# Lightning attention, then a highway layer, on one core: q, k and v loaded in DMAs of 256 KB instead of 128 KB, and five more idle matrix products near the start

## The chip, the cores and the metric

The kernel runs on one NeuronCore of a Trainium2 chip. The metric is the device time of one execution, in microseconds; the kernel before was run three times. A profile of one execution goes with it. Its times are counted from the first instruction, and it names the engines PE (TensorE, matrix products), PEld (TensorE's weight loads), DVE (VectorE), ACT (ScalarE), POOL (GpSimd) and SP (SyncE, which here only issues DMAs). "SPq" and the like mean an engine's sequencer.

## The reference

Four batches, eight heads, 768 positions, 64 features a head. Attention with decay runs over blocks of 64 positions, with a state per batch and head; its output goes through a highway layer of width 512.

```python
for b in range(nb):                      # blocks of 64 positions
    intra = (qb @ kb.T * Dmask) @ vb     # Dmask[i, j] = lam ** (i - j) for i >= j, else 0
    inter = (qb * lam ** (pos + 1)) @ kv_state
    out[block] = intra + inter
    kv_state = lam ** 64 * kv_state + (kb * lam ** (63 - pos)).T @ vb
H = relu(x @ w_h)                        # x: out as [3072, 512]
T = sigmoid(x @ w_t + b_t)
result = T * H + (1 - T) * x
```

## The kernel before

The work is cut into 12 steps: four batches of three steps, each of 256 positions and all eight heads (N = 12, NST = 3). A step is loaded as three float32 tensors q, k and v of 512 KB each (`load`, L205 to L209). Steps 0 and 1 are handled in two parts of four heads, p0 and p1 (`PARTS`, L41); the later ones whole. A partition holds two neighbouring positions, so that one run of a load is 512 bytes of HBM; 128 KB are two heads, 128 partitions each, 256 runs.

The chain of a step is this. Casts to bfloat16 make kb from k (`cast_k`, L212), and qb and vs from q and v with powers of lam multiplied in (`scale`, L215). PE turns kb and qb (`trans`, L220), ACT or DVE copies the turned tiles out of PSUM to kT and qT (`evac_h`, L225). PE makes the scores (`scores`, L233), DVE masks them to m (`mask`, L242). PE multiplies m with vs (`intra`, L257, tile o), adds the share of the state (`inter`, L247, called i0 below for a batch's first step), and advances the state in tile kv (`state`, L268), which ACT or DVE copies to ss (`evac_s`). Tile o is copied to xT (`evac_x`). The highway layer takes xT: eight products with a half of w_h or w_t make one group (`block`, L290, four groups a step), DVE makes hmx (`hmx`, L296), ACT the sigmoid, DVE and POOL the product th (`thmx`, L308). PE turns xT + th back (`turn`, L311), a copy brings it to o_sb, and SP stores it (`store`, L322; 25 stores).

The weights come in eight DMAs of 256 KB (`load_w`, L168) that SP issues after the loads of step 2, and they are cast in pieces of 128 x 512.

`fill` (L196) is an idle product: two matmuls of the identity with 512 columns each into a PSUM tile that no one reads. The kernel issues twelve at the start (`NF`, L40), ahead of the first turn.

What runs where is fixed. Every piece of work is a task with an engine (`FIXED` and `EN`), and `ORDER` lists the tasks; each engine, SP's queue among them, gets its own in that order, one after the other. In SP's queue all loads stand ahead of all stores. Each tensor has a small ring of buffers: five for a step's q, k and v in float32 (`LA`), four for parts, twelve for o_sb (`OB`), three for kb and vs, two for qb.

Of the kernel before, what the change touches and what calls it, by code (L numbers as in the profile page):

```python
# [20 lines left out]
class Task:  # L21
# [15 lines left out]
XB = 3  # L37
OB = 12
WB = 5
NF = 12  # L40
PARTS = 2  # L41
TH = ["DVE", "POOL"]
GROUPS = [[0], [1], [2], [3], [4], [5], [6], [7], [8], [9], [10]]
# [1 line left out]
    cw="GVGGGAAA", ck2="VVGA", cq2="VVGG", cv2="VGVV", et2="VAAVAVAV", ss="AAVAAAAVAVAAAAVVAVAV", xT="VAVAAAAAAAAAAAAAAAAAAAAA",  # L45
    eo="AVVAAAVAAVAVAVAAAAVAVA", ck="VAAGGAGVGG", cq="GVGGGGGGGG", cv="GGGGGGGGGG", et="AVAVAVVAVAAAAAAAAAAA", eo1="A", eo3="AA")
ORDER = [
    34, 32, 20, 33, 21, 43, 22, 42, 23, 16, 44, 24, 25, 26, 83, 27, 35, 17, 28, 82, 37, 29, 30, 36, 92, 31, 46, 38, 40, 93, 39,
    41, 84, 45, 50, 48, 51, 47, 52, 94, 49, 53, 86, 55, 133, 54, 56, 85, 132, 57, 88, 95, 134, 90, 18, 89, 58, 91, 96, 12, 59, 19,
    64, 60, 63, 87, 61, 107, 65, 100, 97, 14, 62, 108, 102, 98, 109, 99, 136, 103, 0, 101, 104, 105, 106, 110, 135, 2, 111, 138,  # L50
    8, 140, 112, 139, 10, 137, 141, 113, 6, 13, 4, 114, 15, 145, 142, 171, 146, 115, 1, 73, 147, 143, 170, 123, 3, 74, 172, 9,
    144, 211, 124, 148, 66, 149, 7, 11, 150, 71, 5, 210, 67, 68, 72, 116, 174, 69, 212, 151, 121, 70, 152, 117, 75, 251, 173, 178,
    122, 118, 153, 179, 176, 175, 119, 250, 154, 177, 120, 79, 76, 155, 214, 252, 185, 77, 80, 180, 161, 181, 186, 184, 213, 187,
    125, 289, 188, 182, 218, 189, 162, 156, 190, 183, 215, 219, 288, 216, 157, 159, 217, 158, 191, 254, 290, 160, 220, 192, 225,
    126, 221, 193, 226, 129, 253, 201, 227, 328, 127, 130, 258, 163, 256, 202, 194, 329, 257, 255, 259, 224, 195, 228, 263, 222,
    330, 229, 196, 292, 223, 230, 260, 264, 197, 231, 370, 164, 261, 291, 232, 265, 167, 233, 199, 198, 165, 293, 369, 262, 168,
    200, 266, 294, 267, 296, 331, 203, 295, 234, 407, 297, 236, 268, 332, 235, 298, 368, 237, 269, 303, 334, 299, 238, 270, 241,
    333, 304, 406, 271, 239, 305, 335, 336, 240, 242, 373, 204, 408, 300, 205, 337, 302, 306, 272, 307, 301, 243, 448, 308, 207,
    338, 273, 372, 208, 343, 309, 344, 339, 447, 277, 310, 345, 311, 274, 410, 278, 446, 279, 275, 244, 371, 280, 276, 319, 487,
    245, 409, 342, 320, 346, 281, 340, 374, 347, 341, 488, 376, 348, 411, 375, 317, 377, 312, 486, 412, 313, 247, 413, 349, 318,  # L60
    450, 81, 378, 248, 381, 350, 314, 379, 351, 382, 414, 449, 315, 206, 383, 352, 415, 451, 316, 282, 380, 353, 283, 249, 384,
    452, 385, 321, 454, 453, 386, 285, 416, 284, 490, 286, 387, 455, 169, 421, 417, 354, 422, 388, 287, 389, 423, 357, 489, 246,
    355, 128, 359, 491, 358, 209, 390, 356, 360, 78, 494, 391, 166, 361, 420, 495, 424, 131, 418, 322, 425, 419, 397, 426, 325,
    323, 492, 398, 326, 324, 362, 427, 327, 493, 456, 461, 395, 457, 428, 462, 429, 365, 463, 363, 460, 396, 366, 364, 464, 458,
    465, 499, 367, 392, 459, 466, 435, 500, 393, 501, 430, 394, 496, 431, 399, 467, 432, 436, 468, 497, 469, 437, 433, 498, 438,
    434, 502, 400, 503, 439, 472, 401, 504, 470, 402, 473, 403, 471, 505, 404, 474, 440, 506, 405, 477, 441, 520, 475, 442, 478,
    507, 476, 443, 509, 508, 479, 444, 512, 510, 521, 445, 513, 514, 511, 523, 522, 515, 480, 483, 524, 516, 481, 528, 484, 526,
    525, 482, 529, 531, 485, 527, 517, 532, 530, 518, 533, 534, 519, 535, 536]


@with_exitstack
def kernel(
# [11 lines left out]
    nc = tc.nc  # L84
    B, H, S, D = q.shape
    C = 128
# [4 lines left out]
    J = 2  # L91
# [48 lines left out]
    def buf(name, tag, shape, dtype=BF16, bufs=1, pool=None):  # L140
        made[name] = Tile(tag, bufs)
        made[name].make = lambda: (pool or sb).tile(shape, dtype, tag=tag, name=tag, bufs=bufs)
        return made[name]

    def get(*key):
        x = made[key]
        if x.obj is None:
            x.obj = x.make()
        return x.obj

    def task(kind, emit, reads=(), writes=(), after=(), only=()):
        eng = FIXED.get(kind)
        if eng is None:
            i = count.get(kind, 0)
            count[kind] = i + 1
            eng = LETTER[EN[kind][i]]
        t = Task(kind, eng, emit, [made[x] for x in reads], [made[x] for x in writes], after, only)
        tasks.append(t)
        return t
# [40 lines left out]
    buf(("fill",), "o", [128, 2, NP, C], F32, pool=ps)  # L200
    for i in range(NF):
        task("fill", fill, writes=[("fill",)])


    def load(x, src, n, p, hs):  # L205
        b, c = divmod(n, NST)
        for h in range(hs.start, hs.stop, 2):
            nc.sync.dma_start(out=get(x, n, p)[:, h - hs.start:h - hs.start + 2, :],  # L208
                              in_=src[b, h:h + 2, c * 2 * C:(c + 1) * 2 * C, :].rearrange("h (p j) d -> p h (j d)", j=J))  # L209


    def cast_k(n, p, hs, eng):  # L212
# [115 lines left out]
    for n in range(N):  # L328
        bt, c = divmod(n, NST)
# [18 lines left out]
        for p, hs in enumerate(parts):  # L348
            z = hs.stop - hs.start
            for x, src in (("k", k), ("q", q), ("v", v)):  # L350
                buf((x + "f", n, p), x + "f" + y, [128, z, J * D], F32, 4 if P2 else LA)
                task("l" + y, lambda eng, x=x, src=src, n=n, p=p, hs=hs: load(x + "f", src, n, p, hs), writes=[(x + "f", n, p)])
            for x in "kq":
                buf((x + "tr", n, p), "w", [128, z // 2, J, C], bufs=WB, pool=ps)
            cast = {}
            cast["k"] = task("ck" + y, lambda eng, n=n, p=p, hs=hs: cast_k(n, p, hs, eng), reads=[("kf", n, p)], writes=[("kb", n)])
            cast["q"] = task("cq" + y, lambda eng, n=n, p=p, hs=hs: scale("qf", get("qb", n).rearrange("p j h d -> p h j d"), pow_q, n, p, hs, eng),
                             reads=[("qf", n, p)], writes=[("qb", n)], after=[pows])
            task("cv" + y, lambda eng, n=n, p=p, hs=hs: scale("vf", get("vs", n), pow_k, n, p, hs, eng), reads=[("vf", n, p)], writes=[("vs", n)], after=[pows])
            for x, xT in (("k", kT), ("q", qT)):  # L360
                task("tr" + y, lambda eng, x=x, n=n, p=p, hs=hs: trans(x, n, p, hs), reads=[(x + "b", n)], writes=[(x + "tr", n, p), xT], only=[cast[x]])
                ev[x, p] = task("et" + y, lambda eng, x=x, n=n, p=p, hs=hs: evac_h(x, n, p, hs, eng), reads=[(x + "tr", n, p)], writes=[xT])
# [111 lines left out]
```

## Time and profile before

| | us |
|---|---|
| runs of the kernel | 127.79, 126.82, 128.57; median 127.79 |
| the profiled execution, its span | 127.79, 126.0 |
| PE busy (share of the span) | 105.4 (84%) |
| DVE, ACT, POOL busy | 78.8, 73.0, 63.6 |
| first load issued, last load issued, first store issued | 0.80, 90.50, 91.06 |
| last store issued | 122.77 |
| DMA | 27.58 MB, mean 219 GB/s |

A busy time counts the engine's own instructions; waiting and issuing are not in it. The end of a matmul is modelled, so a busy PE need not be at its peak. The clock column is the share of full speed that TensorE was granted. A wait is named by what ended it: an engine with its tile and line, or a DMA by its destination and source.

### The profile page before, as it was taken

To read this page: it belongs to the slowest core of one execution; us is meant where nothing else is said; L and a number is where in the kernel's file an instruction comes from. 1 tells how busy PE (TensorE), PEld (TensorE's weight loads), DVE (VectorE), ACT (ScalarE), POOL (GpSimd) and SP (SyncE) were. 2 spreads that over 40 slices of the span, in tenths; PEclk is the share of its full clock that TensorE was granted. 3 is DMA by queue.
4 is the path that set the end of the run, shared out by engine and by line. 5 is a ranking of instruction groups with operands and counts; after the bars stand their busy time and mean duration, and the time that the engine had idled before them with its cause. 6 is when DMAs were issued, how large, how long until landed. Compare 5 with 4: busy or idle time off the path is not lost.

```text
span 126.0 us, 4886 instructions
## 1 busy us (share of the span) xinstructions
PE 105.4 (84%) x2073; PEld 88.3 (70%) x2073; DVE 78.8 (63%) x128; ACT 73.0 (58%) x137; POOL 63.6 (50%) x55
## 2 busy tenths in 40 slices
PE   5983778839999997998499986990999999999960
PEld 1442657726889886887388875890979988889950
DVE  0389648750898995988269624884347498666530
ACT  4831423364278887180596695580666872866770
POOL 6007406075099196953877995419979021030520
PEclk9999755595999999999999999999779999999996
DMA  2989968899888687857887788786899972024253
GB/s 50 259 237 261 265 187 240 230 350 314 237 252 223 193 224 206 240 160 207 243 233 219 224 213 252 219 245 199 241 337 365 380 280 92 0 88 166 88 213 123
DMA packets 45117, 27.58 MB, mean 219 GB/s; under 512 B 2980, under 2 KB 42152, under 8 KB 45096
## 3 DMA queue, kind: packets, MB, share of 16 engines
q1 hardware_dynamic: 44944, 27.27, 72.1%
q8 instruction: 16, 0.26, 0.9%
q14 instruction: 5, 0.04, 0.1%
q10 hardware_dynamic: 152, 0.01, 0.1%
HBM read 20.98 MB, written 6.29 MB: 216 GB/s over the span
## 4 chain that ended last, share of the span: by engine, by line
SPq 35%; PE 29%; DMA 19%; issue 4%; POOL 4%; DVE 4%; ACT 1%; POOLq 1%; DVEq 0%
SPq L208 35%; PE w L293 16%; DMA vf<-in_v_dram 7%; DMA kf<-in_k_dram 5%; DMA w_f<-in_moe_w_t_dram 5%; PE w L315 4%; DMA qf<-in_q_dram 2%; PE w L223 2%; PE o L264 2%; PE w L239 2%; DVE hmx L297 2%; PE kv L272 2%; POOL qb L217 2%; POOL vs L217 1%; PE o L252 1%
## 5 line engine op out<-in xcount | busy, mean ns | idle before, releaser
L293 PE MATMUL w<-xT,w_b 128*128 128x256 bf16 (+1 forms) x416 | 48.9, 271 | 0.4 <-DVE m L243 0.4
L293 PEld LDWEIGHTS <-w_b 128*128 128x128 bf16 x416 | 37.5, 100 | 5.8 <-issue 0.8
L243 DVE TENSOR_TENSOR m<-w,tri 128x512 bf16<-128x512 f32 x48 | 30.7, 685 | 6.0 <-PE w L239 5.8
L217 POOL TENSOR_TENSOR vs<-vf,pow_k 128x1024 bf16<-128x1024 f32 (+1 forms) x11 | 20.1, 1824 | 20.4 <-DMA vf<-in_v_dram 14.3
L309 POOL TENSOR_TENSOR th<-t_sb,hmx 128x512 bf16<-128x512 bf16 (+1 forms) x13 | 14.9, 1144 | 22.1 <-DVE hmx L297 14.8
L217 POOL TENSOR_TENSOR qb<-qf,pow_q 128x1024 bf16<-128x1024 f32 (+1 forms) x11 | 19.2, 1745 | 9.1 <-DMA qf<-in_q_dram 9.1
L297 DVE SCALAR_TENSOR_TENSOR hmx<-w,xT 128x512 bf16<-128x512 f32 (+1 forms) x26 | 16.5, 646 | 6.5 <-PE w L293 6.2
L173 ACT ACTIVATE kT<-w 128x1024 bf16<-128x1024 bf16 (+1 forms) x11 | 10.0, 907 | 11.8 <-PE w L223 11.8
L306 ACT ACTIVATE w<-w,bt_col 128x256 f32<-128x256 f32 (+1 forms) x26 | 11.3, 434 | 8.4 <-PE w L293 6.6
L223 PE MATMUL w<-id,kb 128*128 128x128 bf16 x96 | 8.4, 231 | 8.1 <-POOL kb L175 7.4
L272 PE MATMUL kv<-vs,kb 64*64 64x64 bf16 x320 | 10.6, 203 | 4.4 <-POOL vs L217 3.1
L239 PE MATMUL w<-qT,kT 64*64 64x128 bf16 x384 | 13.1, 232 | 1.4 <-ACT qT L173 0.7
L173 ACT ACTIVATE xT<-o 128x512 bf16<-128x512 f32 x22 | 12.1, 595 | 3.5 <-PE o L264 2.7
L315 PE MATMUL w<-id,th 128*128 128x128 bf16 x96 | 12.9, 220 | 0.6 <-POOL th L309 0.6
L272 PEld LDWEIGHTS <-kb 64*64 64x64 bf16 x320 | 9.0, 116 | 6.0 <-issue 5.8
L306 ACT ACTIVATE t_sb<-w,bt_col 128x256 bf16<-128x256 f32 (+1 forms) x26 | 10.5, 459 | 4.3 <-PE w L293 4.3
L223 PEld LDWEIGHTS <-kb 128*128 128x128 bf16 x96 | 6.2, 103 | 9.7 <-POOL kb L175 8.2
L315 PE MATMUL w<-id,xT 128*128 128x128 bf16 x96 | 12.9, 220 | 0.0
L309 DVE TENSOR_TENSOR th<-w,hmx 128x512 bf16<-128x512 f32 (+1 forms) x13 | 8.4, 649 | 7.0 <-ACT w L306 6.8
L173 ACT ACTIVATE o_sb<-w 128x512 f32<-128x512 f32 (+1 forms) x17 | 9.7, 576 | 4.4 <-PE w L315 4.2
L239 PEld LDWEIGHTS <-kT 64*64 64x64 bf16 x384 | 9.4, 113 | 2.2 <-issue 1.5
L315 PEld LDWEIGHTS <-th 128*128 128x128 bf16 x96 | 9.4, 98 | 0.9 <-POOL th L309 0.8
(46 smaller groups left out, 124.0 us busy)
## 6 DMA issues: line engine op xcount, KB each, us to landing
vf<-in_v_dram SPq DMA_DIRECT2D x48, 128.0 KB, 3.3
kf<-in_k_dram SPq DMA_DIRECT2D x48, 128.0 KB, 3.3
qf<-in_q_dram SPq DMA_DIRECT2D x48, 128.0 KB, 3.0
out_dram<-o_sb SPq DMA_DIRECT2D x23, 256.0 KB, 4.0
w_f<-in_moe_w_t_dram SPq DMA_DIRECT2D x4, 256.0 KB, 5.5
w_f<-in_moe_w_h_dram SPq DMA_DIRECT2D x4, 256.0 KB, 5.7
out_dram<-o_sb SPq DMA_DIRECT2D x2, 128.0 KB, 1.8
lam_bc<-in_lam_dram ACTq DMA_DIRECT2D x1, 4.0 KB, 2.7
```

What stands on the lines that cost most here:

```text
L173: A.activation(dst, src, AF.Copy)
L208: nc.sync.dma_start(out=get(x, n, p)[:, h - hs.start:h - hs.start + 2, :], in_=src[b, h:h + 2, c * 2 * C:(c + 1) * 2 * C, :].rearrange("h ...
L217: ENG[eng].tensor_tensor(dst[:, hs], in0=get(x, n, p).rearrange("p h (j d) -> p h j d", j=J), in1=pw[:, :, :, None].to_broadcast([128, hs. ...
L223: T.transpose(get(x + "tr", n, p)[:, i, j, :], get(x + "b", n)[:, j, h:h + 2, :], id128)
L239: T.matmul(get("s", n, u, e)[half(b), i, j, :], lhsT=turned("k", n)[half(e), hp, b * C + j:(b + 1) * C:J], rhs=turned("q", n)[half(e), hp, ...
L243: V.tensor_tensor(get("m", n, u)[:, e], in0=get("s", n, u, e), in1=tri[:, None].to_broadcast([128, 2, J, C]), op=ALU.mult)
L272: T.matmul(get("kv", n // NST)[half(e), hp, :], lhsT=get("kb", n)[half(b), j, 2 * hp + e, :], rhs=get("vs", n)[half(b), 2 * hp + e, j, :], ...
L293: T.matmul(get(x, g, js[0])[:, i, :], lhsT=w[:, kc, j * 128:(j + 1) * 128], rhs=get("xT", g)[:, kc, :], start=(kc == 0), stop=(kc == KC - 1))
L297: V.scalar_tensor_tensor(get("hmx", g, js[0]), in0=get("h", g, js[0]), scalar=0.0, in1=get("xT", g)[:, js[0]:js[-1] + 1, :], op0=ALU.max, ...
L306: A.activation(get(*gate(g, js))[:, i, :], get("t", g, js[0])[:, i, :], AF.Sigmoid, bias=bt_col[:, j:j + 1])
L309: ENG[TH[js[0] // len(js) % 2]].tensor_tensor(get("th", g)[:, js[0]:js[-1] + 1, :], in0=get(*gate(g, js)), in1=get("hmx", g, js[0]), op=AL ...
L315: T.matmul(get("x", n, b, p)[:, (j - js[0]) * 128:(j - js[0] + 1) * 128], lhsT=get(x, g)[:, j, r * C:(r + 1) * C], rhs=id128, start=(j == ...
```

## The change

Three things differ.

`load` issues one DMA for four heads (256 KB, 512 runs) instead of one for two: 72 loads instead of 144. A part of step 0 or 1 is one DMA, a whole tensor of a later step two.

`NF` is 17 instead of 12. The first twelve fills stand where they did. The five others stand on PE's queue one each after the turns of k part 0, q part 0, q part 1 and k part 1 of step 0, and after the first scores of step 0.

`ORDER` is written anew. The tasks after the fills have numbers that are five higher. Engine by engine, apart from the fills, PE's order is the same. On SP the store of step 2, half 0, goes from the tenth to the fourth place of the stores and that of step 4, half 0, from the seventh to the tenth. On DVE, xT of step 0, half 0, and the copy of the bias go behind the two casts of vs of step 1, one mask of step 1 goes behind the copy of ss and of qT, and four other tasks pass a neighbour. On ACT two tasks and on POOL one task pass a neighbour.

```diff
-NF = 12
+NF = 17
...
 ORDER = [
-    34, 32, 20, 33, 21, 43, 22, 42, 23, 16, 44, 24, 25, 26, 83, 27, 35, 17, 28, 82, 37, 29, 30, 36, 92, 31, 46, 38, 40, 93, 39,
+    39, 37, 20, 38, 21, 48, 22, 47, 23, 16, 49, 24, 25, 26, 88, 27, 40, 17, 28, 87, 42, 29, 30, 41, 97, 31, 51, 43, 32, 98, 44,
+    45, 33, 46, 89, 50, 55, 52, 34, 99, 56, 53, 35, 91, 54, 138, 57, 36, 58, 90, 137, 60, 59, 93, 100, 139, 95, 61, 18, 94, 101,
...
     def load(x, src, n, p, hs):
         b, c = divmod(n, NST)
-        for h in range(hs.start, hs.stop, 2):
-            nc.sync.dma_start(out=get(x, n, p)[:, h - hs.start:h - hs.start + 2, :],
-                              in_=src[b, h:h + 2, c * 2 * C:(c + 1) * 2 * C, :].rearrange("h (p j) d -> p h (j d)", j=J))
+        for h in range(hs.start, hs.stop, 4):
+            nc.sync.dma_start(out=get(x, n, p)[:, h - hs.start:h - hs.start + 4, :],
+                              in_=src[b, h:h + 4, c * 2 * C:(c + 1) * 2 * C, :].rearrange("h (p j) d -> p h (j d)", j=J))
```

## The prediction, written before the result was known

> **What bounds the kernel now.** I read the chain of work that ended last first, then the DMA issues, the DMA queues, and tables by stage.
>
> ```profile
> SPq 35%; PE 29%; DMA 19%; issue 4%; POOL 4%; DVE 4%; ACT 1%; POOLq 1%; DVEq 0%
> ...
> q8 instruction: 16, 0.26, 0.9%
> ...
> vf<-in_v_dram SPq DMA_DIRECT2D x48, 128.0 KB, 3.3
> kf<-in_k_dram SPq DMA_DIRECT2D x48, 128.0 KB, 3.3
> qf<-in_q_dram SPq DMA_DIRECT2D x48, 128.0 KB, 3.0
> ```
>
> The largest share of the chain is SP's sequencer, which only issues. Its timeline says why (columns: start, duration, instruction, count):
>
> ```profile
> 8.99 0.98 SPq L208 DMA_DIRECT2D kf<-in_k_dram  x2
> 10.02 0.98 SPq L208 DMA_DIRECT2D qf<-in_q_dram  x2
> 11.04 2.01 SPq L208 DMA_DIRECT2D vf<-in_v_dram  x4
> 13.09 3.37 SPq L208 DMA_DIRECT2D qf<-in_q_dram  x4
> ```
>
> From 8.99 to 13.09 are eight issues: 0.51 us each, back to back, so 128 KB per 0.51 us, 256 GB/s whatever the DMA engines could do. 144 loads and 8 weight loads make 152 x 0.51 = 78 of the 90 us before the first store (91.06). The other 12 us are long issues as in the last row (3.37 instead of 2.0). Each meets a packet of queue q8, 16 KB of instructions; 0.9% of 16 engines over 126 us is 18.1 us, 1.13 us each. It holds up one DMA engine: in the semaphore times one load lands at 14.90, the next at 17.19, and then the engine that was late catches up, nine landings to 20.61, 0.38 us each. After the weights there are eleven at 0.41 us (31.53 to 36.03). So 128 KB can pass in about 0.40 us.
>
> Next, what TensorE loses. Tables by stage (PE, PEld, DVE, ACT, POOL busy, then clock, DMA share, GB/s), then PE's waits from 27 us on:
>
> ```profile
> 11.07:14.48 3.41, 1.49 (x57) 1.36 (x57) 2.52 (x6) 1.12 (x2) 2.46 (x4) 1.00 0.92 264
> 14.48:24.72 10.24, 8.22 (x168) 6.99 (x161) 7.37 (x11) 3.27 (x6) 2.32 (x2) 0.50 0.80 221
> 31.55:89.58 58.03, 50.35 (x1086) 44.15 (x1080) 40.39 (x61) 36.26 (x66) 39.69 (x26) 1.00 0.79 222
> 89.58:92.99 3.41, 3.41 (x75) 2.71 (x73) 2.29 (x4) 2.37 (x4) 3.41 (x3) 0.50 0.86 258
> 93.00:120.00 27.00, 26.94 (x547) 24.21 (x546) 17.81 (x32) 18.25 (x39) 8.19 (x8) 1.00 0.52 192
> ```
>
> ```profile
> PE w L223 <- POOL kb L175: 5.4, 4, 3.0
> PE kv L272 <- POOL vs L217: 3.1, 2, 2.0
> PE w L239 <- ACT qT L173: 0.7, 1, 0.7
> PE w L293 <- DVE m L243: 0.4, 1, 0.4
> ```
>
> Once the loads are in (93 us), PE is full to 120: PE sets the end. Before that it waits for casts that themselves waited for loads: POOL began kb at 48.94, 56.59 and 87.17 right after k landed, vs at 25.35 and 59.66 right after v. Steps are loaded every 7.3 us (first q issue of step 3 at 25.92, of step 11 at 84.08). PE needs 6.8: turns of k for step 3 at 38.30, for step 8 at 76.42, less 4.3 us of waits between them, over 5. The loads are the slower by 0.5 us a step.
>
> **What the Trainium skill says.** "DMA: Bandwidth & Descriptors", section "Issuing engines are not separate DMA queues": the sequencer's time to start a DMA is usually small beside the DMA. Here it is not: 0.51 against 0.40 us. The same page, "Queues, rings and completion order": an engine takes queue rows in turn, a packet at a time; the q8 packets agree, as each delays a landing. "TensorE: Matmul & The Clock Gate", Part 1: after an idle window of about 3.4 us the array runs at half clock until a busy one. The rows above agree: 1.49 of 3.41 us busy, then 10.24 us at 0.50; and 3.0 us idle at 85 to 88, then 3.41 us at 0.50.
>
> **The change, part by part.**
>
> *Loads.* 72 issues fewer take 72 x 0.51 = 37 us from SP. Bytes, 512-byte runs and run count stay. What an issue with 512 runs costs, the trace doesn't show. Upper bound: in proportion to runs, 1.03 us, and nothing is won. Lower bound: as now, 0.51. For the slope: stores (128 runs) that follow a semaphore wait take 0.33 us at least, loads (256 runs) 0.37, so 0.04 per 128 runs and about 0.6 us for 512. I take 0.6: below the 2 x 0.40 = 0.80 us that the transfer lasts, so the DMA engines become the limit and SP then stalls at no cost. For the transfer I keep 0.38 below and 0.43 above (16 packets of an engine at the median record of 27 ns). A 256 KB load lands as its second half did; steps 2 to 11 wait for all of a tensor anyway, and for steps 0 and 1 a part is now one DMA. No earlier use is lost.
>
> *Landings early on.* First load: 3.93 + 0.40 = 4.33 (its pair: 4.40 now), then 0.80 each. Part k1/p0 (eighth) 9.9 against 12.21; v1/p1 (twelfth) 13.1 against 17.44; with one instruction packet, k2 17.5 against 20.61 and v2 19.1 against 25.19; the weights at 0.72 a piece (as now) and another packet, 25.9 against 31.11.
>
> *Five fills.* Each two products of 512 columns, 0.43 us from start to start at full clock: 2.15 us on PE, between 8.2 and 11.3. The twelve fills already hold PE until 7.99, though kb was ready at 5.87, so these add directly: second scores of step 0 at 11.3 instead of 10.58, DVE's four masks end about 13.5 instead of 12.76. The products of m and vs start at 13.6 instead of 13.70: they now wait for masks where the turns of k of step 1 (12.99, cast waited for its load) used to come. DVE's order also puts two casts of vs (0.69 each) ahead of xT of step 0, so xT ends at 16.1 instead of 15.08 and PE's i0 comes at 16.1 instead of 15.13. Up to here, 1.0 us lost.
>
> *Steps 1 and 2.* Three load waits go: kv of step 1 for vs (DVE idle 1.84, landing 17.44), kb of step 2 (20.61), vs of step 2 (25.19). PE is idle in 12.0 to 16.1 save 1.0 us, so I expect half clock again. On DVE's queue: masks, ss, qT and kb of step 2 end near 20.7 (now 21.64); qT of step 2 near 23.7 (24.85); scores of step 2 23.8 (24.90). POOL ends vs of step 2 at 21.0 (27.25), so kv follows at 24.2 (27.30) and the highway products at 24.7 (27.68). In the kernel before these ran at half clock from 28.14; with the gap gone they run full, and the third product group, at 31.93 now, starts at about 26.9: **5.0 us gained**. At full clock throughout, 25.8 (6.1); if DVE's queue slips, 28.5 (3.4).
>
> *Steps 3 to 11.* A step is supplied every 12 x 0.40 + 1.13 = 5.9 us, below PE's 6.8 and even at 0.43 (6.3): from step 3 the loads run ahead, with 5 buffers each. PE's waits of the list, 9.6 less 2.0 for kv of step 2 already counted: **7.6 us**. The half clock at 89.58 to 92.99, half of 3.41: **1.7 us**. New waits: POOL becomes dense, two casts of 1.90, kb 1.04 and th 1.15 = 6.0 of 6.8 us; followed through its queue from th of step 0, kb of step 8 ends near 65 and PE wants it at 67.6, so nothing stops, but the slack is thin. I add 1.0 us. Loads end near 74; the stores follow, twelve o_sb buffers against a 13th write near 83. The tail, 121.3 to 126.0, stays.
>
> *Other moves.* On SP the store of step 2, half 0, stands fourth instead of tenth, that of step 4, half 0, tenth instead of seventh; all stores stay behind all loads, and step 2's was turned at 54.5: nothing. On DVE, ACT and POOL ten instructions pass a neighbour or two (mask of step 1 behind ss, which I used above; q of step 11 ahead of a th): I count nothing, since PE's lead over them hides it; where a neighbour is late one instruction's time is lost, 0.4 to 1.9 us, which is within the 1.0 us and the first rival.
>
> Sum on the profiled span: 126.0 - 5.0 - 7.6 - 1.7 + 1.0 = 112.7. The profiled execution took 127.79, 1.8 us more than its span, and 127.79 is also the median of the three runs: 112.7 + 1.8 = **114.5 us**.
>
> **Rivals.** The forecast above has 0.51. *The early queues give less* (chance 0.2): fills and the moved xT hold DVE, the shift is 2 to 3 us and POOL's queue adds 1 more: 117.5 to 119. For it: DVE busy 7.37 of 10.24 us in that stage. *DMA limits more* (0.15): instruction packets cost the queue 2 us each, as the 14.90 to 17.19 gap did, giving 4.8 + 2.3 = 7.1 a step, above 6.8; the 7.6 us are then won by half: 118. Against it: catching up. *All early work at full clock, no new waits* (0.1): 126.0 - 6.1 - 7.6 - 1.7 + 1.8 = 112.4. *Issue in proportion to runs* (0.04; not faster): at L208 an issue of 1.03 us keeps 256 GB/s, and the fills' 1.0 us stands: 128 to 129. It decides from 0.95 us per issue (12 x 0.475 + 1.13 = 6.8). Against it: the 0.33 and 0.37.
>
> **How the numbers follow.** A measurement here tells about 2%. Faster by more: all cases but the last, 0.95; within 2%: 0.03; slower 0.02 (fills without any gain). The likeliest case alone spans 113 to 116.5 (shift 6.1 to 3.4 us, new waits 0.5 to 1.5). The range runs from 111, the full-clock case with landings at 0.38 (36 x 0.02 = 0.7 less up to v2) and the spread of the runs shown (126.82 to 128.57), to 119, which holds both middle rivals.
>
> **What would show it.** Right: 72 loads at 0.8 us from issue to issue, above 300 GB/s until about 30 us; last load landed near 74; no PE wait on kb or vs after 30 us; no half clock near 90. Wrong: issues of 1.0 us with DMA share as now; PE waiting on POOL though loads have landed; i0 far behind 16 us.

## The result and the profile after

The kernel after took 111.84 us (median of four runs, 111.70 to 112.25), beside 127.31 us for the kernel before in turn with it on the same chip: ratio 0.882, with a 95% interval of 0.874 to 0.890. Its profiled execution took 111.97 us, with a span of 110.2. Here and below a time is the median of all runs of a kernel, while a ratio with its interval rests on the runs within 1.5% of a kernel's fastest.

On the page of the kernel after, these rows answer to the chain by engine and to the DMA issues (their count, size, median us from issue to landing):

```profile
PE 71%; SPq 12%; DMA 6%; POOL 5%; issue 1%; DVE 1%; POOLq 1%; ACT 0%
...
vf<-in_v_dram SPq DMA_DIRECT2D x24, 256.0 KB, 6.0
kf<-in_k_dram SPq DMA_DIRECT2D x24, 256.0 KB, 5.5
qf<-in_q_dram SPq DMA_DIRECT2D x24, 256.0 KB, 5.4
```

SP's sequencer has gone from 35% of the chain to 12%, and PE from 29% to 71%. A load takes longer from issue to landing (5.4 to 6.0 us instead of 3.0 to 3.3): it carries twice the bytes and, with the DMA engines kept busy, stands in their queue. SP's timeline of the kernel after shows the two kinds of issue:

```profile
1.30 0.51 SPq L208 DMA_DIRECT2D kf<-in_k_dram  x1
1.86 1.05 SPq L208 DMA_DIRECT2D qf<-in_q_dram  x2
2.95 1.43 SPq L208 DMA_DIRECT2D kf<-in_k_dram  x1
...
10.58 1.71 SPq L208 DMA_DIRECT2D qf<-in_q_dram  x2
12.33 1.71 SPq L208 DMA_DIRECT2D kf<-in_k_dram  x2
```

The second to fourth, with little in the queue yet, take 0.51 us each (0.55 from start to start), although each carries 512 runs. Later it is 0.88 us from one to the next (10.58 to 12.33 for two), at a DMA share above 1.1: SP is held up by the transfer. The stages of the kernel after, with columns as before (PE, PEld, DVE, ACT, POOL busy, clock, DMA share, GB/s), and its PE waits from 24 us on:

```profile
11.07:14.48 3.41, 2.71 (x80) 1.83 (x81) 3.02 (x6) 1.33 (x3) 2.40 (x3) 1.00 1.22 290
14.48:24.00 9.52, 6.29 (x220) 5.11 (x209) 8.31 (x15) 4.93 (x9) 4.15 (x3) 1.00 1.11 299
31.00:90.00 59.00, 58.76 (x1341) 52.48 (x1339) 46.60 (x73) 45.41 (x81) 46.80 (x31) 1.00 0.99 288
```

```profile
PE w L315 <- POOL th L309: 0.6, 1, 0.6
PE w L223 <- POOL kb L175: 0.2, 1, 0.2
```

From 31 to 90 us PE is busy in 58.76 of 59.00; in the kernel before it was 50.35 of 58.03 over about the same stretch. The waits for kb, vs and qT are gone but for 0.2 us. What the DMA engines moved rose from 222 to 288 GB/s (284 from 31 to 72 us, while only loads were issued).

### The profile page after: what moved, and what is told of

Its sections match the earlier page's. It is cut to its first block, busy times and chain, and to the rows that moved or that the text cites. A ratio compares the mean times of both kernels' runs of the same rounds, so it can differ in the third digit from the quotient of the medians.

```text
span 110.2 us, 4797 instructions
## 1 busy us (share of the span) xinstructions
PE 100.9 (91%) x2083; PEld 84.4 (77%) x2083; DVE 78.5 (71%) x128; ACT 73.2 (66%) x137; POOL 63.9 (58%) x55
## 4 chain that ended last, share of the span: by engine, by line
PE 71%; SPq 12%; DMA 6%; POOL 5%; issue 1%; DVE 1%; POOLq 1%; ACT 0%
PE w L293 37%; SPq L208 12%; PE w L315 9%; PE w L223 8%; DMA vf<-in_v_dram 6%; PE o L264 5%; PE w L239 4%; PE kv L272 4%; PE o L252 3%; POOL vs L217 2%; POOL qb L217 2%; POOL kb L175 1%; DVE hmx L297 1%; POOLq L469 1%; ACT o_sb L173 0%
## 5 line engine op out<-in xcount | busy, mean ns | idle before, releaser
L293 PE MATMUL w<-xT,w_b 128*128 128x256 bf16 (+1 forms) x416 | 46.9, 265 | 0.0
L293 PEld LDWEIGHTS <-w_b 128*128 128x128 bf16 x416 | 36.6, 98 | 4.3
L309 POOL TENSOR_TENSOR th<-t_sb,hmx 128x512 bf16<-128x512 bf16 (+1 forms) x13 | 15.0, 1155 | 20.3 <-DVE hmx L297 13.3
L306 ACT ACTIVATE w<-w,bt_col 128x256 f32<-128x256 f32 (+1 forms) x26 | 11.3, 434 | 6.1 <-PE w L293 4.8
L239 PE MATMUL w<-qT,kT 64*64 64x128 bf16 x384 | 11.7, 220 | 0.6 <-DVE qT L175 0.6
L198 PE MATMUL o<-id 128*128 128x512 bf16 x34 | 10.0, 439 | 1.4 <-POOL id masks.py:199 1.4
L272 PE MATMUL kv<-vs,kb 64*64 64x64 bf16 x320 | 9.4, 194 | 0.4 <-DVE ss L175 0.3
L315 PEld LDWEIGHTS <-xT 128*128 128x128 bf16 x96 | 9.3, 98 | 0.5
L239 PEld LDWEIGHTS <-kT 64*64 64x64 bf16 x384 | 8.3, 106 | 1.6 <-issue 1.3
L223 PE MATMUL w<-id,kb 128*128 128x128 bf16 x96 | 7.7, 220 | 1.9 <-DVE kb L175 1.5
```

Of the source, the lines that this page charges most:

```text
L223: T.transpose(get(x + "tr", n, p)[:, i, j, :], get(x + "b", n)[:, j, h:h + 2, :], id128)
L239: T.matmul(get("s", n, u, e)[half(b), i, j, :], lhsT=turned("k", n)[half(e), hp, b * C + j:(b + 1) * C:J], rhs=turned("q", n)[half(e), hp, ...
L272: T.matmul(get("kv", n // NST)[half(e), hp, :], lhsT=get("kb", n)[half(b), j, 2 * hp + e, :], rhs=get("vs", n)[half(b), 2 * hp + e, j, :], ...
L293: T.matmul(get(x, g, js[0])[:, i, :], lhsT=w[:, kc, j * 128:(j + 1) * 128], rhs=get("xT", g)[:, kc, :], start=(kc == 0), stop=(kc == KC - 1))
L306: A.activation(get(*gate(g, js))[:, i, :], get("t", g, js[0])[:, i, :], AF.Sigmoid, bias=bt_col[:, j:j + 1])
L309: ENG[TH[js[0] // len(js) % 2]].tensor_tensor(get("th", g)[:, js[0]:js[-1] + 1, :], in0=get(*gate(g, js)), in1=get("hmx", g, js[0]), op=AL ...
```

## The experiments

They ran on two chips. The comparison of twelve with seventeen fills and the two runs with mixed sizes ran on one, where the kernel before takes 128.93 us and the kernel after 112.76; all others on another, where it is 129.0 and 112.61. "Before" and "after" below are meant on the same chip.

**Each part alone.** First the loads without the fills:

```diff
-NF = 17
+NF = 12
```

(with the five fills struck from `ORDER`.)

> The kernel after with the five extra fills taken out (twelve stay), 256 KB loads kept. Theory 'issue' (the time came from SP's issues alone): 110.5 to 113 us, that is between 1.3 us faster than the kernel after, if the fills only held back step 0, and 1 us slower, if PE falls to half clock for a stretch in steps 1 and 2 and that is partly hidden. Theory 'clock' (the fills, by keeping TensorE at full clock, brought most of it): 117 us or more, with 10 us or more at half clock, since the kernel before spent 17 us at half clock.

Measured: 113.11 us, 0.890 of before (0.886 to 0.894), with 10.2 us at half clock: 0.1 above the range of the first theory, and far below the second's. Then the fills without the loads:

```diff
-        for h in range(hs.start, hs.stop, 4):
+        for h in range(hs.start, hs.stop, 2):
```

(and the slices likewise.)

> The kernel after with loads of 128 KB again, the five fills and the new order kept. Theory 'issue': 126 to 129 us as before, 0.51 us from issue to issue, first store near 91 us; the fills may save or cost 1 us. Theory 'clock': 121 us or less, with no long half clock after 14 us.

Measured: 128.35 us, 0.992 of before (0.984 to 0.999), first store at 90.7. So the loads carry the gain but for about 1 us. Both runs keep the new order, so this 1 us is that of the fills and the order together; the large loads in the old order were not run. Whether the fills add anything to them was left open by the 113.11, so the kernel with twelve fills and the kernel after ran once more, in turn:

> 256 KB loads, twelve fills, once more, in turn with the kernel after on the same chip. If the five fills bring what the first run of this kernel seemed to show: 0.3 to 1.3 us above the kernel after, with 10 us at half clock. If that was scatter between runs: within 0.3 us of it.

> The kernel after unchanged, as the partner of the run with twelve fills: 111.7 to 112.7 us; which end of this depends on when TensorE first gets full clock (4 to 7 us after the start) and on 0 to 7 us at half clock in steps 1 and 2.

Measured: 112.95 us (0.876, 0.870 to 0.882) with twelve, 112.76 (0.8755, 0.870 to 0.881) with seventeen, no difference that stands out of the scatter (112.16 to 114.20 and 112.06 to 113.71). The stages 8 to 13 and 13 to 24 us, twelve fills first, then seventeen, show why:

```profile
8.00:13.00 5.00, 3.04 (x55) 1.95 (x54) 4.23 (x9) 2.05 (x5) 2.88 (x3) 0.99 1.22 290
13.00:24.00 11.00, 10.06 (x217) 8.65 (x216) 8.66 (x15) 4.84 (x10) 5.24 (x4) 0.54 1.14 309
```

```profile
8.00:13.00 5.00, 5.00 (x70) 2.84 (x67) 3.88 (x8) 2.15 (x5) 2.60 (x3) 1.00 1.20 291
13.00:24.00 11.00, 9.02 (x225) 7.66 (x226) 9.46 (x16) 4.92 (x10) 4.88 (x4) 0.69 1.14 309
```

The fills do fill PE (5.00 of 5.00 instead of 3.04), and the clock in the next stage is better, 0.69 instead of 0.54. But in that stage PE is not what the rest waits for: it has room at either clock (10.06 and 9.02 of 11.00 us busy). Loads and casts set the pace: v of step 2 landed at 21.41 with twelve fills and 21.40 with seventeen, POOL's cast of it ended at 23.44 and 23.43, and the highway products began at 24.81 and 24.40.

**Other places for the fills.** Two runs put the five fills where PE has been idle, the second with nine in front instead of twelve (`ORDER` alone is changed, and `NF`):

> 256 KB loads and 17 fills as in the kernel after, but the five extra ones stand where PE has been idle: two ahead of the turns of k part 1, one ahead of the second scores of step 0, one ahead of the first turns of step 1, one ahead of the first product of m and vs. Theory 'fills work by keeping the clock': time follows the share of half clock and not the fills' places; 111.3 to 112.3 with a mean clock of 0.96 or more, up to 113 where it falls to 0.95. Theory 'their places cost time': first scores of step 0 about 0.4 us earlier than 11.0 and the whole 0.4 us or more below the kernel after.

> As the run with the fills in the gaps, but nine instead of twelve at the start (14 in all), so the first turns can start near 7.0 instead of 8.3. Theory 'the first fills hold the path': about 0.7 us faster than the kernel after. Theory 'step 1 and 2 wait for their loads in any case' (v of step 1 landed at 15.12, k of step 2 at 19.78): within 0.5 us of it, unless the clock falls to half, which costs up to 1.3.

> The kernel after unchanged, beside the two runs with other places of the fills on the same chip: 111.5 to 112.5 us, half clock for 0 to 7 us of the first 25.

Measured: 112.31 us (five in the gaps), 112.72 (nine in front), 112.61 (after, which like the 112.76 above is 0.1 over its expected range), their ratios to before 0.888, 0.895 and 0.891 with overlapping intervals. The first scores of step 0 did come earlier, at 10.29 in the first of them, as the second theory there said, but the time did not follow; within the runs of these kernels the lower times went with the higher clock (111.56 and 111.77 at 1.00, 112.99 at 0.979). Neither theory's number for the first of them stands out of the scatter of about 1 us. The reason the time did not follow can be read from the traces: v of step 2 landed at 21.63 (21.59 in the kernel after), and the highway products began at 24.74 (24.75). With nine in front the gain of 0.7 us that the first theory there had did not come; within 0.5 us, as the second had it, is what was measured. None of these beats the kernel after.

**Fewer, larger DMAs still.** One DMA of 512 KB for each whole tensor (`h` in steps of `hs.stop - hs.start`):

> The kernel after with one DMA of 512 KB for a whole tensor of steps 2 to 11 (parts of steps 0 and 1 stay at 256 KB): 42 loads instead of 72. Theory 'DMA engines and PE are now the limit': within 1 us of the kernel after, landings still about 0.44 us per 128 KB, SP's issues only longer. Theory 'SP still limits in part': 1 us or more faster.

Measured: 112.50 us (0.887, 0.881 to 0.894), like the kernel after. So at 256 KB SP's issuing is no limit any more. One row of SP's timeline in that kernel prices the issue: 1024 runs, after a wait, in 0.37 us, where the others are held up for longer.

```profile
22.26 0.37 SPq L209 DMA_DIRECT2D qf<-in_q_dram  x1
22.96 1.81 SPq L209 DMA_DIRECT2D kf<-in_k_dram  x1
...
58.60 3.73 SPq L209 DMA_DIRECT2D vf<-in_v_dram  x2
```

**More, smaller DMAs.** One head, 64 KB, in a DMA:

```diff
-        for h in range(hs.start, hs.stop, 4):
+        for h in range(hs.start, hs.stop, 1):
```

> The kernel after with loads of 64 KB (one head): 288 loads. Theory 'issue': 0.51 us per issue whatever its size, 296 x 0.51 = 151 us until the first store, and then the rest of the last steps on PE, 20 to 35 us: 170 to 187 us. Theory 'an issue's cost follows its runs or bytes': 0.26 us per issue, so 126 to 130 us as with 128 KB.

Measured: 193.25 us, ratio 1.522 (1.509 to 1.535). SP's timeline there:

```profile
61.01 3.75 SPq L208 DMA_DIRECT2D kf<-in_k_dram  x8
64.81 3.77 SPq L208 DMA_DIRECT2D vf<-in_v_dram  x8
```

Eight issues in 3.80 us, 0.475 each, for half the bytes. The table by stage, from 20 to 150 us, has the DMA engines busy for half of the time (share 0.49):

```profile
20.00:150.00 130.00, 73.53 (x1323) 61.23 (x1318) 50.40 (x77) 44.61 (x82) 46.67 (x32) 0.79 0.49 136
```

The first store came at 157.67; with 128 KB it was 91.06, so 144 more issues cost 66.6 us, 0.46 each. The count sets it and not the bytes. The time lies 6 us above the top of my 170 to 187: the first store came 6.7 us later than my 151, since I had added nothing for issues that are held up or wait (which the kernel before has too, 12 us of them). The rest after the first store took 34 us of span, within my 20 to 35.

**Where in the kernel the gain is made.** Large loads early and small ones late, and the reverse:

```diff
+        z = 4 if n < 3 else 2
-        for h in range(hs.start, hs.stop, 4):
+        for h in range(hs.start, hs.stop, z):
```

(with the slices likewise; the other run has `2 if n < 3 else 4`.)

> The kernel after with loads of 256 KB in steps 0 to 2 and of 128 KB from step 3 on. Theory 'two gains': the early shift is won and then lost again, since from step 3 on a step is supplied every 7.3 us and PE needs 6.8. The last q is issued some 58 us after the first q of step 3 (22.4 in the kernel after), near 80.6 against 84.1 before, so only about 3.5 us of the gain is left: 123 to 126 us. Theory 'the early stage carries the gain': 118 us or less.

> The kernel after with loads of 128 KB in steps 0 to 2 and of 256 KB from step 3 on. Theory 'two gains': the third group of highway products starts near 31 as it does with 128 KB throughout, instead of 26.6; from there PE has no waits and no half clock: 4 to 5 us over the kernel after, 116 to 118 us. Theory 'the early stage carries the gain': 121 us or more.

Measured: 124.64 us (0.967, 0.955 to 0.978) and 116.40 us (0.905, 0.898 to 0.911), both as the theory of two gains had it. PE's waits from 24 us on, large loads early, and its stage 31 to 90:

```profile
PE w L224 <- POOL kb L175: 4.6, 3, 2.8
PE kv L273 <- POOL vs L218: 2.0, 2, 1.4
```

```profile
31.00:90.00 59.00, 50.53 (x1109) 44.00 (x1108) 39.86 (x61) 37.56 (x66) 42.41 (x28) 0.97 0.81 230
```

The same stage with large loads late:

```profile
31.00:90.00 59.00, 59.00 (x1314) 52.55 (x1313) 46.87 (x72) 44.15 (x80) 47.79 (x32) 1.00 1.08 299
```

With small loads late, a step is supplied every 7.2 us (first q of step 3 at 22.55, of step 11 at 80.20), PE waits for kb and vs again and falls to half clock once more at 84.7 for 3.4 us; with large ones it waits for neither. Small early loads cost 3.6 us (116.40 less 112.76), small late ones 11.9 (124.64 less 112.76). Together that is 15.5 of the 16.2 us between before and after on this chip; in the ratios, 0.029 and 0.091 of 0.1245. The profiles keep the two apart: the third group of highway products began at 27.04 us in the kernel after, at 27.54 with small late loads and at 30.80 with small early ones, and from there to the end it took 83.4, 94.2 and 83.4 us.

**Small loads from two sequencers.** Half of the q loads of steps 3 to 11 moved from SP to ACT, in the kernel before:

```diff
-            nc.sync.dma_start(...)
+            eng = nc.scalar if x == "qf" and n > 2 and h < 4 else nc.sync
+            eng.dma_start(...)
```

> The kernel before, 128 KB loads and 12 fills, with half of the q loads of steps 3 to 11 (18 DMAs) issued by ACT instead of SP. Theory 'the issuing sequencer was the limit': SP then supplies a step in 10 x 0.51 + 1.13 = 6.3 us, below PE's 6.8, first store 7 to 9 us earlier, and most of PE's 7.6 us of waits and the 1.7 us of half clock go: 118 to 122 us, ACT's 18 x 0.5 us of issuing taking part of it. Theory 'a DMA of 128 KB moves its bytes more slowly than one of 256 KB' or 'the DMA engines were the limit': 126 to 130 us.

Measured: 136.44 us, ratio 1.082 (1.070 to 1.094), slower, which neither theory had. The first store was issued at 86.19, 4.9 us earlier than in the kernel before, so SP did gain. But ACT's own waits, by what ended them, were these:

```profile
ACT xT L173 <- DMA kf<-in_k_dram: 7.5, 1, 7.5
ACT o_sb L173 <- DMA qf<-in_q_dram: 5.5, 1, 5.5
...
ACT xT L173 <- DMA qf<-in_q_dram: 4.5, 1, 4.5
```

A copy of xT has no need of a k in flight: what waited was the load ahead of it on ACT's queue. ACT's timeline shows the first of the three waits:

```profile
24.90 0.63 ACT L173 ACTIVATE w_b<-w_f 128x512 bf16<-128x512 f32 x1 [0.16 <-DMA w_f<-in_moe_w_t_dram]
31.75 1.25 ACTq L209 DMA_DIRECT2D qf<-in_q_dram  x2
33.06 0.60 ACT L173 ACTIVATE xT<-o 128x512 bf16<-128x512 f32 x1 [7.53 <-DMA kf<-in_k_dram]
```

From 25.53 us on ACT did nothing until the first of its two loads for step 3 went out at 31.75, 0.02 us after a load of k had landed. Its buffer was free (the second of five), so it waited for that landing and not for a buffer. In the two other waits as well, each load went out 0.02 to 0.03 us after another load had landed. Why it was made to wait for an earlier DMA (a semaphore that both use would do it) stays open. The Trainium skill, "DMA: Bandwidth & Descriptors", says in its section "Anatomy of one DMA — SWDGE (gpsimd) path" that DMA engines do not wait on semaphores and that any such wait happens on the issuing sequencer, before dispatch. That section is about DMAs issued from GpSimd; these rows show the same on ACT. SP can stand there at no cost, ACT cannot: 17.5 us in three waits.

So this run says nothing for or against SP's issues as the limit; the runs with 64 KB, and with mixed sizes, do. The rival that a DMA of 128 KB moves its bytes more slowly than one of 256 KB does not fit the landings in the kernel before: where loads were queued they landed 0.38 and 0.41 us apart (17.19 to 20.61, 31.53 to 36.03), no slower than the 0.88 us of 256 KB in the kernel after.

## Why the prediction was right, point by point

*The bound.* SP's issues at 0.51 us were the limit until the last load: shown by the 64 KB run (0.46 us for each further issue) and by the 512 KB run (no gain from fewer still). The stated rival of an issue in proportion to its runs is out: 0.51 us for 512 runs in the kernel after, 0.37 for 1024 after a wait. I had taken 0.6. One reading in the prediction was too simple: of the 12 us beyond the 0.51 us an issue, ten long issues at packets of q8 make 9.7 (0.73 to 1.36 each). Most of the rest, 2.7 us, is loads of step 3 that waited for the weights to land, and one packet (at 30.29) held up none.

*The transfer* was mis-sized. I took 0.80 us for 256 KB from landings that followed a held-up engine, with 0.86 as the upper end; with the queue kept full it is 0.88, and the first load landed at 5.18 instead of 4.33. So landings came later than written: k of step 1, part 0, at 11.49 (9.9), v of step 2 at 21.45 (19.1), the last weights at 27.36 (25.9), the last load at 78.7 (74), and from 11 to 24 us the rate was 290 to 299 GB/s and not above 300. In the later steps it cost nothing: q of step 3 was issued at 22.41 and q of step 11 at 68.09, 5.7 us a step, below the 6.7 that PE takes (turns of k for step 3 at 32.93, for step 8 at 66.54). That 5.7 lies so near my 5.9 is luck. The bytes take 6 x 0.88 = 5.3 us instead of 4.8, and only 0.4 us of the 1.13 that I charged for an instruction packet is left.

*The first steps.* The second scores of step 0 came at 11.89 (11.3), m times vs at 13.40 (13.6). i0 was at 15.33 and not 16.1: I had let it wait for xT, as the trace before names it, but here xT waits for i0 (until 15.76) and i0 for ss. So 0.2 us were lost where I had 1.0. Half clock was expected in steps 1 and 2 and did not show in this profile, which is luck: in the repeats it shows for 3 to 7 us, and costs less than those runs scatter by (of the four runs above, the one with a mean clock of 0.969 took 112.25 us, the others, at 1.00, 111.70 to 111.97). The "idle window" that the prediction sets ahead of half clock is only partly idle here: in the kernel before PE was busy for 1.49 us of the 3.41 from 11.07 and for 1.32 of the 3.41 from 86.17. kv of step 2 followed its vs (POOL 21.59 to 23.49, forecast to end at 21.0) at 23.54 (24.2), and the third group of highway products began at 26.55 (26.9): 5.4 us of shift against 5.0.

*The later steps.* Waits: 7.6 us expected to go, 7.4 went. The half clock near 90 us went (1.7). New waits: 1.0 expected, 0.2 seen; kb of step 8 was indeed the tight one, ready at 66.49 (65), and held PE up for the 0.2. From the third group to the start of the last turn it was 89.2 us before (31.93 to 121.16) and is 79.3 now (26.55 to 105.89), 9.9 less where my terms give 8.3. Of that 1.6, 0.8 is the wait that I added and that didn't come; the rest fits what an emptied PE adds to each of seven waits: its matmuls overlap by some 0.15 us, and the waits are counted from the end of the one before. That is argued from the durations, not run.

*The tail* was 4.8 us and is 4.3, as the last store landed sooner. Sum: 5.4 + 9.9 + 0.5 = 15.8 us of span, 126.0 to 110.2; I had 13.3. Of the 2.5 us between them, 1.6 lie in the later steps, 0.5 in the tail, for which I had forecast nothing, and 0.4 in the early shift. The forecast of 114.5 was 2.7 us high and within its range. A slip in the rival of the early queues changes nothing: its terms give 117.5 to 118.5, not 119.

*The split* is confirmed in kind by the two runs with mixed sizes, and less in size: small early loads cost 3.6 us where I had 5.0, small late ones 11.9 where I had 8.3. The fills, which with the moved xT I had charged with 1.0 us in step 0, come out at nothing on either side.

## What to carry to other kernels

When the chain runs through an issuing sequencer, divide the bytes of one DMA by the time from issue to issue: if that rate is below what the DMA engines reach elsewhere in the same trace, put more bytes into each DMA, and stop where the sequencer begins to be held up by the transfer. Compare the supply per step with the bounding engine's need per step in the same units (7.3 against 6.8 us here, then 5.7 against 6.7): here a deficit of half a microsecond at every step cost more than all that the start lost. Idle products that keep an engine's clock up were worth nothing that could be measured here, where loads and casts set the pace of their stage.

## What I had not expected of the hardware

With the queue kept full, loads in runs of 512 bytes moved at 290 GB/s (11.07 to 14.48 us in the kernel after). The weights, loads in runs of 1 KB, landed 0.72 us apart for 256 KB in the kernel before, which is 364 GB/s, and stores, in runs of 2 KB, reached 372 GB/s (95 to 100 us there). A packet of 16 KB of instructions takes 0.9 to 1.6 us in the kernel after. TensorE first got full clock between 4.1 and 7.3 us after the start, so the last of the same first twelve idle products began anywhere from 7.78 to 9.26 us.
